# First in-projection of blocks 2 and 3: column tiles 4 to 15 as three groups of seven products, with stores, loads and conversions moved

## The chip, the cores and the metric

The program runs on one core of one Trainium2 chip. Its engines run side by side, each with a queue of its own: TensorE (PE) multiplies, VectorE (DVE), ScalarE (ACT) and GpSimd (POOL) do elementwise work, and SyncE (SP) issues the transfers. The metric is the device time of one execution in microseconds; of several runs the median counts. A time below is one on the span of the profiled execution, from its start, unless it is said to be otherwise.

## The reference

Attention with an exponentially decaying state (retention), then an MLP with a squared ReLU, then a gated MLP on normalized rows, all in float32:

```python
for t in range(S):
    state = gamma[None, :, None, None] * state + np.einsum('bhd,bhe->bhde', k[:, :, t], v[:, :, t])
    y[:, :, t] = scale * np.einsum('bhd,bhde->bhe', q[:, :, t], state)
...
h = np.maximum(x @ w_in, 0.0)              # x: 3072 x 512, w_in: 512 x 2048
x = h * h @ w_out
...
rms = np.sqrt(np.mean(x * x, axis=-1, keepdims=True) + 1e-06)
xn = x / rms * rms_g
g = xn @ w_gate                            # 512 x 1536
silu = g * (1.0 / (1.0 + np.exp(-g)))
val = xn @ w_val
return silu * val @ w_out
```

## The kernel before

The 3072 tokens go in six blocks of 512, each of four chunks of 128. A float32 matrix product is made of three passes: every operand is split into a high part (a cast on ACT, `split`, L103) and a low part (a subtraction on DVE, `low`, L100), and PE adds high x high, high x low and low x high (`mm3`, `proj`). One such pass over 128 rows and 512 tokens is one matmul of 128x512.

Block 0 and block 1 go through the first MLP one by one (`block1`). Blocks 2 and 3 go through it together, and so do 4 and 5. For a pair of blocks the in-projection is written in two ways. `in_phase` takes a column tile of 128 columns after the other: 12 matmuls for each of the two blocks, then ReLU and square on ACT. `in_pair` takes four column tiles together as a 2x2 scheme (two halves of the input dimension, two blocks) with seven products P1 to P7 for eight: each product is 12 matmuls too, its weights are a unit of 512 KB (a sum or difference of quarters of the weights, high and low part), and its other operand is one of seven combinations X[P1] to X[P7] of the blocks (`first_x` makes them, two at 128x1024 for each: a cast `xop` on ACT, a low half on DVE, with differences `raw<-raw` on DVE between them). DVE then adds what a product gives to several results: `act<-pr` behind P2, `act<-ph` or `act<-pb` behind P7, `act<-pa` behind P3. With NCL = 4, column tiles 0 to 7 are plain, and 8 to 15 are the groups 2 and 3.

Units are made once: weights arrive as 64-bit numbers (`raw`), are converted (`tick`: a magnitude on ACT, L228, and two integer operations on DVE, L233 and L234), split, and stored to DRAM as they are (`keep_units`, `keep_in`: P1, P2, P4) or as sums (`made_units`: P5, P7, P6, P3, a `made` tile each, cast on ACT, low half on DVE, stored by SP). `in_units` makes those of the in-projection, in the order of groups 2, 3, 0, 1; for groups whose rows were stored (`rows_i`) it reads them back, for the others it adds the high and low parts (`whole_rows`, four sums on DVE). `ring` is a ring of seven tiles into which SP loads the units ahead of the products that use them. Almost all of these tiles (`w`, `raw`, `rows`, `made`, `wps`, `ring`, `xop`, `act`) come from one pool of 38 places of 4 KB a partition: a new tile takes the place of an old one and waits until all that reads or writes the old one is done, a store of it included.

Between the products of blocks 2 and 3, the eight attention chunks of blocks 4 and 5 are computed, one at each visit (`visit`, L1038): a state product (into the last columns of bank `pr`, L992; not for the last four chunks), values into `pr` (L1003, L1012), and the scores of the next chunk into a pair of free banks (L957). Around a visit ACT copies `pr` out (`raw<-pr`), DVE adds the state (`st<-st,pr`), POOL decays the state and the next values and queries (L1023, L945, L934), and DVE masks the scores (`causal`, L975 and L980), which the next visit multiplies. In `in_phase` there is a visit behind the second block of each odd column tile; in `in_pair` one behind P6 and one behind P3.

The order is written out by hand: `after1` (L1407) says what follows each half of a column tile, `after1b` (L1423) what follows each product, `late0`, `late1` and `last1` what lies in `block1`. There is no planner; the names of the places where work is put are the generators `made_in` (units), `coming_xs` (X), `back` (norm) and the list `later` (stores), which are advanced by a step at a time. SP and the engines take their queues strictly in that order.

In the gated MLP, `make_late` (L1623) makes units of the last out-projection the same way, beside the first pair of blocks.

## Time and profile before

| | us |
|---|---|
| median of 3 runs (1086.36 to 1087.31) | 1086.46 |
| the profiled execution | 1087.08 |
| its span, first to last instruction | 1085.4 |
| PE busy | 1077.3 |
| DVE busy | 792.4 |
| ACT busy | 571.7 |
| POOL busy | 76.5 |
| in-projection of blocks 2 and 3, from and to | about 228 to 336 |

A wait is put down to the engine whose signal came last. A row of a timeline gives the start, the time of the instruction, the engine (SPq: SyncE's queue), the line and the operation as result<-operands with its shape; in square brackets stands how long the engine was idle before it and who ended that. The start of one row less the start of the row before is the engine's pitch, which is shorter than the time of one instruction, since the next begins before the last has quite ended.

### The profile page before, as it was taken

The numbers are of one execution on the slowest core, as the hardware profiler recorded it, in microseconds if no ns is written. First come the engines' busy times: TensorE is split into PE (matmuls) and PEld (weight loads), VectorE is DVE, ScalarE is ACT, GpSimd is POOL, SyncE is SP. The second block draws the span as 40 slices with busy tenths as digits, with TensorE's granted clock in tenths as the row PEclk, the third lists the DMA queues.
The fourth block names the chain that finished last, engine by engine and source line by source line (L and its number), as shares of the span: only waits on it lengthen the run. The fifth ranks groups of instructions, "written<-read, shape, count | busy, mean of one in ns | idle before, by whom it ended". The sixth has DMA issues, their size and how long they took to land. (4 is left out here: it accounts for less than half of the span.)

```text
span 1085.4 us, 16696 instructions
## 1 busy us (share of the span) xinstructions
PE 1077.3 (99%) x6281; PEld 887.2 (82%) x6281; DVE 792.4 (73%) x1103; ACT 571.7 (53%) x880; POOL 76.5 (7%) x65
## 2 busy tenths in 40 slices
PE   8999999999999999999999999999999999999998
PEld 7788888888888888888888887888888888888887
DVE  6988678888758995679788887995333896433585
ACT  5777445567566557785455655453333554233442
POOL 3000143314310000000000000000000000000000
PEclk9999999999999999999999999999999999999999
DMA  9868799899999779976569979767567567555563
GB/s 359 324 213 318 242 319 383 307 383 342 395 408 349 252 276 378 375 275 247 197 230 337 377 277 365 272 208 237 194 233 250 194 212 251 194 194 195 194 213 117
DMA packets 108452, 300.87 MB, mean 277 GB/s; under 512 B 11044, under 2 KB 34364, under 8 KB 108372
## 3 DMA queue, kind: packets, MB, share of 16 engines
q1 hardware_dynamic: 108192, 299.56, 76.5%
q8 instruction: 50, 0.82, 0.3%
q10 hardware_dynamic: 180, 0.24, 0.1%
q14 instruction: 30, 0.25, 0.1%
HBM read 211.14 MB, written 88.62 MB: 276 GB/s over the span
## 5 line engine op out<-in xcount | busy, mean ns | idle before, releaser
L492 ACT CAST o<-act 128x1024 fp32r<-128x1024 f32 x101 | 105.5, 1051 | 110.1 <-DVE act L107 55.8
L100 DVE TENSOR_TENSOR o<-act,o 128x1024 fp32r<-128x1024 f32 x101 | 123.0, 1222 | 25.9 <-ACT o L492 25.9
L270 PE MATMUL ph<-o,ring 128*128 128x512 f32 x228 | 88.9, 390 | 0.0
L271 PE MATMUL ph<-o,ring 128*128 128x512 f32 x228 | 88.6, 389 | 0.0
L269 PE MATMUL ph<-o,ring 128*128 128x512 f32 x228 | 88.6, 389 | 0.0
L311 PE MATMUL ph<-xh,w_i 128*128 128x512 f32 x248 | 81.2, 390 | 0.0
L269 PE MATMUL ph<-xop,ring 128*128 128x512 f32 x192 | 75.4, 393 | 1.1 <-ACT part L114 1.0
L269 PE MATMUL pa<-xop,ring 128*128 128x512 f32 x192 | 75.0, 391 | 0.0
L269 PE MATMUL pb<-xop,ring 128*128 128x512 f32 x192 | 74.9, 390 | 0.0
L270 PE MATMUL ph<-xop,ring 128*128 128x512 f32 x192 | 74.9, 390 | 0.0
L271 PE MATMUL ph<-xop,ring 128*128 128x512 f32 x192 | 74.8, 390 | 0.0
L271 PE MATMUL pa<-xop,ring 128*128 128x512 f32 x192 | 74.8, 390 | 0.0
L270 PE MATMUL pb<-xop,ring 128*128 128x512 f32 x192 | 74.8, 390 | 0.0
L271 PE MATMUL pb<-xop,ring 128*128 128x512 f32 x192 | 74.8, 389 | 0.0
L270 PE MATMUL pa<-xop,ring 128*128 128x512 f32 x192 | 74.8, 389 | 0.0
L107 DVE TENSOR_TENSOR act<-act 128x1024 f32<-128x1024 f32 x60 | 73.3, 1221 | 0.3
L110 DVE TENSOR_TENSOR part<-pr,part 128x512 f32<-128x512 f32 x38 | 25.7, 690 | 52.5 <-ACT part L114 51.2
L770 ACT ACTIVATE t<-part 128x512 f32<-128x512 f32 x54 | 34.1, 632 | 49.7 <-DVE part L110 49.7
L114 ACT COPY part<-ph 128x512 f32<-128x512 f32 x52 | 29.9, 587 | 52.7 <-PE ph L271 52.7
L311 PEld LDWEIGHTS ph<-xh,w_i 128*128 128x128 f32 x248 | 46.5, 188 | 10.2 <-ACT w_o L132 0.4
L270 PEld LDWEIGHTS ph<-o,ring 128*128 128x128 f32 x228 | 42.8, 188 | 9.6 <-DVE o L100 0.9
L269 PEld LDWEIGHTS ph<-o,ring 128*128 128x128 f32 x228 | 42.8, 188 | 8.9
(255 smaller groups left out, 2624.6 us busy)
## 6 DMA issues: line engine op xcount, KB each, us to landing
ring<-wu SPq DMA_DIRECT2D x84, 512.0 KB, 4.3
ring<-up SPq DMA_DIRECT2D x63, 512.0 KB, 4.3
ring<-uo SPq DMA_DIRECT2D x56, 512.0 KB, 3.8
ring<-ui SPq DMA_DIRECT2D x42, 512.0 KB, 7.0
wu<-ring SPq DMA_DIRECT2D x42, 512.0 KB, 6.7
raw<-w1i SPq DMA_DIRECT2D x16, 512.0 KB, 6.9
raw<-w1o SPq DMA_DIRECT2D x16, 512.0 KB, 8.4
vkt<-vk SPq DMA_DIRECT2D x16, 512.0 KB, 6.0
```

Of the source, the lines that this page charges most:

```text
L100: eng.tensor_tensor(out=dst_l, in0=src, in1=dst_h.bitcast(F32), op=ALU.subtract)
L107: eng.tensor_tensor(out=out_, in0=a, in1=b, op=ALU.subtract)
L110: eng.tensor_tensor(out=out_, in0=a, in1=b, op=ALU.add)
L114: nc.scalar.copy(dst[:, m], acc[m])
L269: nc.tensor.matmul(acc, ah, bh, start=start, stop=False, **more)
L270: nc.tensor.matmul(acc, ah, bl, start=False, stop=False, **more)
L271: nc.tensor.matmul(acc, al, bh, start=False, stop=stop, **more)
L311: nc.tensor.matmul(h, w[:, a, k * 128:(k + 1) * 128], x[b][k], start=n == 0, stop=n == len(order) - 1)
L492: nc.scalar.copy(h, src)
L770: nc.scalar.activation(t, g, AF.Silu)
```

## The change

NCL becomes 2: column tiles 0 to 3 stay plain, 4 to 15 become the groups 1, 2 and 3. `KEPT` takes over what NCL said of the weights that are stored on their way (still tiles 8 to 15). With it move:

- the unit stores: `keep_out` begins at column tile 5 of block 0 (was 8), `keep_in` at tile 12 of block 0 (was tile 0 of block 1);
- the units: `in_units` goes 1, 2, 3, 0 (was 2, 3, 0, 1), so the rows of group 1 are summed from high and low part first;
- the ring's first loads: from tile 13 of block 1 (RING_AT, was behind the blocks), and behind both halves of a plain tile;
- the conversions: from tile 11 of block 1 (MORE_AT, was 12), in `in_phase` none at tile 2 and none ahead;
- the X operands: `first_x` makes P6 and P5 before P7, advances at both halves of tiles 2 and 3, and behind P1, P2 and P6 of the first group;
- the last units of the gated MLP: at its next to last group of the first pair of blocks `make_late` makes no step behind P5 and three behind P6 (were one and two).

```diff
--- before.py
+++ after.py
@@ -39,14 +39,15 @@
 COMING = (0, 1, 2, 5, 8, 9, 13, 16, 17, 18, 19, 20)
 AHEAD = 5
 EARLY = 24
-MORE_AT = 12
+MORE_AT = 11
 W2_SOON = 25
 X_AT = (11, 12, 17, 18, 23, 24)
 
 P2, P1, P5, P6, P7, P3, P4 = range(7)
 PQ = 128 // CB
-NCL = 4
-RING_AT = 16
+KEPT = 4
+NCL = 2
+RING_AT = 13
 EPS = 1e-06
 WARM = 10
 GAMMA = (1.0 - 2.0 ** (-5.0 - np.arange(H))).astype(np.float32).astype(np.float64)
@@ -76,7 +77,7 @@
     uo2 = [[dram.tile([128, 2, 512], F32, name=f"up{q}{k}") for k in range(7)] for q in range(NQ2)]
     wu = [[dram.tile([128, 2, 512], F32, name=f"wu{n}{k}") for k in range(7)] for n in range(NPR)]
     rows2 = [[dram.tile([128, 2, 512], F32, name=f"rows_p{q}{r}") for r in range(2)] for q in range(NQ2)]
-    kept = {(k, n): dram.tile([128, 2, 512], F32, name=f"rows_{k}{n}") for k in "io" for n in range(NCL, 2 * NQ)}
+    kept = {(k, n): dram.tile([128, 2, 512], F32, name=f"rows_{k}{n}") for k in "io" for n in range(KEPT, 2 * NQ)}
 
     ones = const.tile([128, D], F32, name="ones")
     g_sb = const.tile([128, KC], F32, name="g_sb")
@@ -130,7 +131,7 @@
         t = slot(f"w_{key[0]}{key[1]}", F32R)
         W[key] = t
         nc.scalar.copy(t[:, 0, :], f)
-        if key[1] >= 2 * NCL:
+        if key[1] >= 2 * KEPT:
             nc.sync.dma_start(kept[key[0], key[1] // 2][:, key[1] % 2, :], f)
         return lambda: low(eng or nc.vector, t[:, 1, :], f, t[:, 0, :])
 
@@ -221,7 +222,7 @@
             key = steps[i][1]
             if key[0] == "p":
                 sizes[i] = row_of(key[1])
-            elif key[0] in "io" and key[1] >= 2 * NCL and i % 3 == 0:
+            elif key[0] in "io" and key[1] >= 2 * KEPT and i % 3 == 0:
                 sizes[i] = tp.tile([128, TB], F32, tag="y", name="f")
             else:
                 sizes[i] = cf.tile([128, 512], F32, tag="f", name="f")
@@ -617,17 +618,17 @@
         yield
         sub(y[0, 0], y[0, 1], y[0, 0])
         yield
+        sub(y[0, 1], y[1, 1], y[0, 1])
+        yield
+        sub(y[1, 1], y[1, 1], y[0, 0])
+        yield
+        X[P6] = put(y[1, 1])
+        yield
         X[P5] = put(y[0, 0])
         yield
-        sub(y[0, 1], y[1, 1], y[0, 1])
+        sub(y[1, 0], y[1, 0], y[1, 1])
         yield
         X[P7] = put(y[0, 1], True)
-        yield
-        sub(y[1, 1], y[1, 1], y[0, 0])
-        yield
-        X[P6] = put(y[1, 1])
-        yield
-        sub(y[1, 0], y[1, 0], y[1, 1])
         yield
         X[P4] = put(y[1, 0], True)
         yield
@@ -1249,13 +1250,13 @@
                 prev = (f, s, j)
 
         def request(key, q):
-            if 2 * q >= NCL and q < NQ:
+            if 2 * q >= KEPT and q < NQ:
                 row_tiles[key, q] = [slot("rows") for _ in range(2)]
                 for r in range(2):
                     nc.sync.dma_start(row_tiles[key, q][r], kept[key, 2 * q + r])
 
         def whole_rows(key, q):
-            if 2 * q >= NCL:
+            if 2 * q >= KEPT:
                 yield
                 return
             rows = row_tiles[key, q] = [slot("rows") for _ in range(2)]
@@ -1280,6 +1281,12 @@
         def keep_out(f):
             keep_units(uo, f, W[("o", f)])
 
+        def keep_in(f):
+            q, r, m = f // 4, f % 4 // 2, f % 2
+            w = W[("i", f)].bitcast(F32)
+            for k, h in ((P1, 0), (P2, 1)) if r == 0 else ((P4, 1),):
+                nc.sync.dma_start(units(ui[q][k])[:, m], w[:, :, h * HALF:(h + 1) * HALF])
+
         made = all_units()
 
         def early0(f):
@@ -1289,8 +1296,10 @@
         def late0(f):
             stores()
             tick(low_first=at[0] < 5)
-            if f >= 8:
-                keep_out(f - 8)
+            if f >= 5:
+                keep_out(f - 5)
+            if f >= NF1 - 4:
+                keep_in(f - NF1 + 4)
 
         nxt = Operand(True)
         block1(0, cur, lambda c: nxt, (3, 7, 11, 14), early0, late0)
@@ -1299,19 +1308,13 @@
         cur = nxt
 
         def in_units():
-            for q in (2, 3, 0, 1):
+            for q in (1, 2, 3, 0):
                 yield from whole_rows("i", q)
                 spare = cf.tile([128, 512], F32, tag="f", name="sm")
                 for n, _ in enumerate(made_units(ui, q, row_tiles.pop(("i", q)), lambda: spare, True)):
                     if n == 1:
                         request("i", q + 1)
                     yield
-
-        def keep_in(f):
-            q, r, m = f // 4, f % 4 // 2, f % 2
-            w = W[("i", f)].bitcast(F32)
-            for k, h in ((P1, 0), (P2, 1)) if r == 0 else ((P4, 1),):
-                nc.sync.dma_start(units(ui[q][k])[:, m], w[:, :, h * HALF:(h + 1) * HALF])
 
         xs, raws1 = [], []
         made_in = in_units()
@@ -1332,9 +1335,10 @@
                 next(made, None)
 
         def late1(f):
-            if f < 8:
-                keep_out(f + 8)
-            keep_in(f)
+            if f + NF1 - 5 < NF1:
+                keep_out(f + NF1 - 5)
+            if f + 4 < NF1:
+                keep_in(f + 4)
             if f % 2:
                 next(made, None)
 
@@ -1354,8 +1358,6 @@
                 more_steps(W2_SOON)
             if f > MORE_AT:
                 tick()
-            if f == 2:
-                request("i", NCL // 2)
             if f >= 4:
                 next(made_in, None)
             if f in (10, 12, 14):
@@ -1407,17 +1409,18 @@
         def after1(f, t):
             if t == 0:
                 stores()
-                tick(ahead=f < 8)
+                if f != 2:
+                    tick(ahead=False)
                 if f and f % 2 == 0:
                     next_chunk()
             elif f % 2:
                 kv, _ = visit(at_chunk, pa, True)
                 after_visit(at_chunk, sink2(at_chunk), kv)
-            if t:
+            if t or f > 1:
                 next(coming_xs, None)
             if f % 2 == 0 or t == 0:
                 next(made_in, None)
-            if t and f and len(ring) < 7:
+            if (t or f) and len(ring) < 7:
                 more_ring()
 
         def after1b(n, k):
@@ -1433,14 +1436,14 @@
                 after_visit(at_chunk, sink2(at_chunk), kv)
             if k in (P1 if n < NQ - 1 else P2, P5, P7, P4):
                 next(made_in, None)
+            if n == NCL // 2 and k in (P1, P2, P6):
+                next(coming_xs, None)
             if n == NQ - 1 and k in (P2, P6, P3):
                 i = (P2, P6, P3).index(k)
                 out_1.hi(i)
                 out_1.lo(i)
 
         in_phase(xs, lambda f: W[("i", f)], after1, between1)
-        for _ in coming_xs:
-            pass
         for n in range(NCL // 2, NQ):
             in_pair(n, after1b)
         for a in last_square:
@@ -1635,7 +1638,7 @@
 
                 def second():
                     nonlocal coming
-                    make_late(1 if p == NPR - 3 else 2)
+                    make_late({NPR - 3: 1, NPR - 2: 3}.get(p, 2))
                     if p == 0 and due:
                         sums(pb[1])
                     background()
@@ -1656,7 +1659,7 @@
                         next(coming, None)
                         next(coming, None)
 
-                pair(s, p, first, lambda: make_late(1), second, third)
+                pair(s, p, first, lambda: make_late(int(p < NPR - 2)), second, third)
 
             def store(dh, t, y):
                 nc.sync.dma_start(out[2 * s + t, dh], y)
```

Three places in the engines' order, as the programs have it. A name's number is that of a buffer. First **DVE, from column tile 3's visit to the add behind P2 of the first group**. Before (the first group is that of tiles 8 to 11, so the column tile ahead of it is 7):

```order
L100 TENSOR_TENSOR xop<-raw,xop 128x1024
L975 TENSOR_TENSOR causal<-pa_226,seen_sb 128x4x64
L980 TENSOR_TENSOR causal<-pa_226,seen_sb 64x2x64 x2
L975 TENSOR_TENSOR causal<-pa_227,seen_sb 128x4x64
L980 TENSOR_TENSOR causal<-pa_227,seen_sb 64x2x64 x2
L233 TENSOR_SCALAR f<-f 128x512
L234 SCALAR_TENSOR_TENSOR f<-raw,f 128x512
L107 TENSOR_TENSOR rows<-rows,sm 128x2x256
L100 TENSOR_TENSOR made<-sm,made 128x2x256
L110 TENSOR_TENSOR act<-pr_232,act 128x512
L110 TENSOR_TENSOR act<-pr_233,act 128x512
```

After (the first group is that of tiles 4 to 7):

```order
L108 TENSOR_TENSOR raw<-raw 128x1024
L976 TENSOR_TENSOR causal<-pa_226,seen_sb 128x4x64
L981 TENSOR_TENSOR causal<-pa_226,seen_sb 64x2x64 x2
L976 TENSOR_TENSOR causal<-pa_227,seen_sb 128x4x64
L981 TENSOR_TENSOR causal<-pa_227,seen_sb 64x2x64 x2
L101 TENSOR_TENSOR wps<-rows,wps 128x512
L234 TENSOR_SCALAR rows<-rows 128x512
L235 SCALAR_TENSOR_TENSOR rows<-raw,rows 128x512
L101 TENSOR_TENSOR made<-rows,made 128x2x256
L101 TENSOR_TENSOR xop<-raw,xop 128x1024
L111 TENSOR_TENSOR act<-pr_232,act 128x512
L111 TENSOR_TENSOR act<-pr_233,act 128x512
```

The add into `act` stood behind one conversion, one difference and one made unit; now a weight row's low half (`wps`) and an x operand's (`xop`) stand there too, and the x operand that stood ahead of the mask is a difference.

In the same place **ACT**, with the engines and transfers (DMAHW) whose signal each row waits for, before:

```order
L302 COPY raw<-pr_232 128x2x128 [waits PE_49]
L302 COPY raw<-pr_233 128x2x128 [waits PE_49]
L103 CAST xop<-raw 128x1024 [waits DVE_49]
L114 COPY act<-ph_230 128x512 [waits PE_49]
L114 COPY act<-ph_231 128x512 [waits PE_49]
L103 CAST made<-sm 128x2x256 [waits DVE_49]
L114 COPY act<-ph_230 128x512 [waits DMAHW1_49,PE_49]
L114 COPY act<-ph_231 128x512 [waits PE_49]
```

and after:

```order
L303 COPY raw<-pr_232 128x2x128 [waits PE_49]
L303 COPY raw<-pr_233 128x2x128 [waits PE_49]
L115 COPY act<-pb_228 128x512 [waits DVE_49,PE_49]
L115 COPY act<-pb_229 128x512 [waits PE_49]
L104 CAST wps<-rows 128x512 [waits DMAHW6_49]
L229 ACTIVATE rows<-raw 128x512
L104 CAST made<-rows 128x2x256 [waits DVE_49,Activation_49]
L104 CAST xop<-raw 128x1024
L104 CAST xop<-raw 128x1024 [waits DVE_49]
```

The cast of the made unit still waits for DVE, and it is followed by two x operands (X[P7], X[P4]).

Then **SP, around the store of the low and high half of a weight row (`up_154<-wps`)**, at column tile 3; before:

```order
L1344 DMA ring_2933<-ui_99 128x1024
L147 DMA up_146<-wps 128x2x256
L147 DMA up_152<-wps 128x2x256
L199 DMA rows_p_209<-rows 128x1024
L199 DMA rows_p_210<-rows 128x1024
L217 DMA raw<-w2g 128x1024
L1344 DMA ring_2995<-ui_98 128x1024
L147 DMA up_154<-wps 128x2x256
L158 DMA ui_86<-made 128x1024
```

and after:

```order
L218 DMA raw<-w2g 128x1024
L1348 DMA ring_2883<-ui_95 128x1024
L913 DMA qnt<-qT 128x512
L918 DMA kTt<-kT 128x512
L905 DMA vkt<-vk 128x1024
L1348 DMA ring_2951<-ui_96 128x1024
L148 DMA up_154<-wps 128x2x256
L1348 DMA ring_2982<-ui_97 128x1024
L159 DMA ui_107<-made 128x1024
L159 DMA ui_109<-made 128x1024
```

Three ring loads stand around that store in place of one.

Last **DVE, from P6's visit to the add behind P3 of the second group** of the new program, which is the first of the old one; before:

```order
L233 TENSOR_SCALAR f<-f 128x512
L234 SCALAR_TENSOR_TENSOR f<-raw,f 128x512
L100 TENSOR_TENSOR made<-rows,made 128x2x256
L110 TENSOR_TENSOR act<-ph_230,act 128x512
L110 TENSOR_TENSOR act<-ph_231,act 128x512
L233 TENSOR_SCALAR f<-f 128x512
L234 SCALAR_TENSOR_TENSOR f<-raw,f 128x512
L110 TENSOR_TENSOR act<-pa_226,act 128x512
L110 TENSOR_TENSOR act<-pa_227,act 128x512
```

and after:

```order
L234 TENSOR_SCALAR f<-f 128x512
L235 SCALAR_TENSOR_TENSOR f<-raw,f 128x512
L108 TENSOR_TENSOR sm<-sm,rows 128x512
L101 TENSOR_TENSOR made<-rows,made 128x2x256
L111 TENSOR_TENSOR act<-ph_230,act 128x512
L111 TENSOR_TENSOR act<-ph_231,act 128x512
L234 TENSOR_SCALAR f<-f 128x512
L235 SCALAR_TENSOR_TENSOR f<-raw,f 128x512
L108 TENSOR_TENSOR rows<-rows,sm 128x2x256
L101 TENSOR_TENSOR made<-sm,made 128x2x256
L111 TENSOR_TENSOR act<-pa_226,act 128x512
L111 TENSOR_TENSOR act<-pa_227,act 128x512
```

Three steps of made units have come in: two differences and a low half.

## Rows read from the trace of the kernel before

**Rows 1.** the page, part 1: busy us (share of the span) xinstructions, by engine

```profile
PE 1077.3 (99%) x6281; PEld 887.2 (82%) x6281; DVE 792.4 (73%) x1103; ACT 571.7 (53%) x880; POOL 76.5 (7%) x65
```

**Rows 2.** waits of PE: engine, line, who ended it: us in total, times, longest

```profile
PE ph L957 <- DMA stage<-qk: 1.4, 1, 1.4
...
PE pr L1003 <- issue: 0.2, 1, 0.2
```

**Rows 3.** windows: us, then each engine's busy us, clock, DMA share and GB/s

```profile
100.00:228.00 128.00, 128.00 (x1174) 105.54 (x1173) 99.17 (x169) 67.33 (x121) 36.47 (x28) 1.00 0.88 316
228.00:288.00 60.00, 60.00 (x539) 49.24 (x538) 52.69 (x83) 39.54 (x70) 18.43 (x13) 1.00 0.97 361
```

**Rows 4.** line L311: its matmuls on x operands, ns min/median/max, first and last

```profile
L311 PE MATMUL ph<-xop,w_i x192: 387/390/500, 228.8 to 284.4; 128*128 128x512 f32 x192
```

**Rows 5.** timeline of PE, two products of the second group

```profile
325.51 0.39 PE L269 MATMUL pb<-xop,ring 128*128 128x512 f32 x1
...
328.23 0.39 PE L269 MATMUL pa<-xop,ring 128*128 128x512 f32 x1
```

**Rows 6.** timeline of PE, the visit at column tile 3

```profile
256.47 0.69 PE L992 MATMUL pr<-vkt 128*64 128x64 f32 x16
...
258.45 0.85 PE L957 MATMUL pa<-qnt,kTt 64*64 64x128 f32 x32
259.23 0.96 PE L311 MATMUL ph<-xop,w_i 128*128 128x512 f32 x3
```

**Rows 7.** timeline of DVE, column tiles 2 and 3 and behind that visit

```profile
252.67 1.79 DVE L100 TENSOR_TENSOR made<-sm,made 128x512 fp32r<-128x512 f32 x1
254.39 1.21 DVE L107 TENSOR_TENSOR raw<-raw 128x1024 f32<-128x1024 f32 x1
255.52 0.68 DVE L107 TENSOR_TENSOR sm<-sm,rows 128x512 f32<-128x512 f32 x1
...
259.70 0.42 DVE L110 TENSOR_TENSOR st<-st,pr 128x256 f32<-128x256 f32 x1
...
261.82 0.41 DVE L975 TENSOR_TENSOR causal<-pa,seen_sb 128x256 f32<-128x256 f32 x1
...
263.10 0.60 DVE L980 TENSOR_TENSOR causal<-pa,seen_sb 64x128 f32<-64x128 f32 x2
```

**Rows 8.** timeline of POOL, the same stretch

```profile
252.31 1.61 POOL L408 TENSOR_TENSOR y<-y 128x512 f32<-128x512 f32 x1 [1.17 <-ACT y L405]
...
263.01 1.04 POOL L945 TENSOR_TENSOR vkt<-vkt,vdec_sb 128x512 f32<-128x512 f32 x1
```

**Rows 9.** timeline of ACT, column tiles 3 to 7

```profile
257.12 0.62 ACT L103 CAST made<-sm 128x512 fp32r<-128x512 f32 x1 [0.93 <-DMA rows_p<-rows]
...
259.33 1.06 ACT L103 CAST xop<-raw 128x1024 fp32r<-128x1024 f32 x1
...
286.01 0.68 ACT L228 ACTIVATE f<-raw 128x512 f32<-128x512 f32 x1 [2.63 <-DMA wq<-f]
```

**Rows 10.** timeline of DVE, the old first group, P5 to P3

```profile
302.80 0.43 DVE L233 TENSOR_SCALAR f<-f 128x512 int32<-128x512 int32 x1 [2.21 <-ACT f L228]
...
303.88 0.68 DVE L100 TENSOR_TENSOR made<-rows,made 128x512 fp32r<-128x512 f32 x1
...
306.86 1.28 DVE L110 TENSOR_TENSOR act<-pa,act 128x512 f32<-128x512 f32 x2
```

**Rows 11.** timeline of PE, the visits behind its P6 and P3

```profile
296.16 1.21 PE L1003 MATMUL pr<-causal,vkt 128*64 128x128 f32 x16 [0.22 <-issue]
...
308.47 0.85 PE L957 MATMUL pa<-qnt,kTt 64*64 64x128 f32 x32
```

**Rows 12.** timeline of all engines, gated units, behind P6 of the fifth group

```profile
653.40 0.63 ACT L103 CAST made<-rows 128x512 fp32r<-128x512 f32 x1
...
653.92 1.08 ACT L114 COPY part<-ph 128x512 f32<-128x512 f32 x2
...
654.57 0.50 PE L269 MATMUL ph<-xop,ring 128*128 128x512 f32 x1 [0.96 <-ACT part L114]
```

4 lines of the change are left out of this document (2 added, 2 removed).

## The prediction

> **What bounds the kernel now.** I read the engines' busy time first [rows 1]: TensorE (PE) is busy 1077.3 of 1085.4 us, VectorE (DVE) 792.4. Then PE's waits [rows 2]: the longest in the whole span is 1.4 us, at its start, and in the stage that changes the only one is 0.2 us. So a matmul less is time less, a wait of PE more is time more, and nothing later gives it back. Then the stage itself, the in-projection of blocks 2, 3, in a window over its column tiles, beside one over the block before [rows 3]: PE runs without a gap in both; DVE is busy 52.69 of 60 us while the column tiles run, and the DMA engines are all but full (0.97). The reader should see three resources there: PE sets the end, DVE has an eighth of its time left, the DMA queue hardly any. The question is whether the gain on PE survives on those two.
>
> The sum is made against the profiled execution's 1087.08 us (span 1085.4 and 1.68 around it); the median of the three runs is 0.62 lower, and I take that off at the end. A measurement of this kernel can tell 0.2%, 2.2 us, from no change, so "same" is 1084.3 to 1088.6.
>
> **The matmuls.** Column tiles 4 to 7 go: 4 tiles, 2 token blocks, 12 matmuls each, 96 of the 192 of [rows 4]. Seven products of 12 come: 84. Twelve matmuls take 2.72 us (325.51 to 328.23, [rows 5]), so **-2.72**. The eight visits of attention chunks stay, with 2.85 us each where a state is added (a turn of 0.09, then 256.47 to 259.23, [rows 6]); two of them move from column tiles 5 and 7 to behind P6 and P3 of the new first group.
>
> **The path to the first visit of the new group.** Let V be the end of the visit at column tile 3 (259.23 before). P1, P2 and P6 follow, and then a visit that writes the banks pr, which DVE must have read (the add of P2 into `act`) by V + 3 x 2.72 + 0.09 = V + 8.25. The visit carries a state, whose first matmuls write pr's second bank, so both halves of the add must be done.
>
> What DVE has queued ahead of that add is in the order of the changed kernel: the last rows are difference, mask, low half of a weight row, conversion, low half of a made unit, low half of an x operand, add. Before, the state's add started at V + 0.47, at 259.70 [rows 7]. Between the first column visit's mask and it the change puts one more x operand and one more difference (1.13 each at DVE's pitch, 254.39 to 255.52) and takes away one conversion with its low half (1.65): 0.6 later, so I put it at V + 1.0. Then 0.34 for it, 1.13 difference, 1.88 mask (261.82 to 263.70), 0.60 low half, 1.14 conversion (1.08 at its pitch, [rows 10]): V + 6.1. ScalarE (ACT) may write the high half of the made unit only now: its tile takes the place of the raw weights that the conversion reads, and its row in the order waits for DVE. That high half and the x operand's behind it take 1.6 (0.52 and 1.06, [rows 9, 12]): V + 7.7. Low half of the operand 1.13, add 1.29: V + 10.1. PE waits 1.9 us, with nothing in the way.
>
> Two things are in the way in this very stage. DVE and GpSimd (POOL) hold each other up: a low half that takes 0.68 took 1.79 (252.67) while POOL's sum of the norm ran [rows 7, 8], so 1.1; in this stretch POOL has a state, two decays and the last sum of the norm. I take two of 1.1: +2.2. And ACT waits for transfers, 0.93 and 2.63 us [rows 9]: a tile is overwritten only when its store has landed. SyncE's queue now has three 512 KB unit loads within five entries of such a store, where it had one, on DMA engines that are all but full. I take one wait like the longer: +2.6. So **+6.7**. Below it, the bare work: from the first column visit's state to the add DVE has 19.4 us at its pitch, and PE needs 48 matmuls, a visit and three products, 21.9 us, so with no wait at all it is 0. Above, two more holds: 8.9.
>
> The Trainium skill, GPSIMD Engine Reference, section Specifications, says that GpSimd shares its SBUF interfaces with VectorE and meets DVE instructions that have two SBUF inputs. By that all four POOL operations of the stretch would find one, 4.4 instead of 2.2, and the sum would be 2.2 us higher. The trace agrees in part: the decay at 263.01 ran its 1.04 beside the last masks, which read a bank of PSUM, and neither was held, so I stay with two.
>
> **P3 of the first group.** The scores of the visit behind P3 write banks pa, which DVE reads in the add behind P3. From the end of the visit before, PE needs 3 x 2.72 and 2.07 (258.45 less 256.47, and the turn): 10.23. DVE has state 0.34, norm 0.2, mask 1.88, low half 0.60, conversion 1.05, two unit-row sums 1.2, add 1.2, conversion 1.05, two sums 1.2, add 1.29: 10.0, begun 0.47 behind the visit, so it ends 0.25 late where all else fits. Before, the scores had 0.33 us to spare (307.50 + 0.64 against 308.47) after 2.21 us of idle DVE [rows 10, 11]. One hold of 1.1 makes it **+1.3**; bounds 0 and 2.5.
>
> **The second group.** Behind its P6, PE was held 0.38 us already (296.16, where the matmul before had ended its turn at 295.78, [rows 11]). DVE has one conversion and one sum more there (1.05, 0.72) and no x operand (1.13): +0.6. Up to its P3 DVE has three made-unit steps more, 1.8 us; the 2.21 us that it idled was a wait for ACT, which converts only when PE's P5 has been read, so it doesn't cover them, and the spare 0.33 does: +1.2 with some luck on ACT's side. Together **+1.8**, bounds 0.3 and 3.5.
>
> **The gated units, 300 us later.** At 654.57 PE waits 1.0 us because ACT casts a made unit before it empties bank ph [rows 12]. The change moves that cast behind both copies; ACT's pitch for one is 0.52 (653.40 to 653.92). **-0.5**, bounds -1.1 and 0.
>
> **At nothing.** Unit stores, ring loads and conversions that move into the blocks before: PE is busy 128.00 of 128 us there [rows 3] and waits for none of them; DVE's four sums for the new group's unit rows, 2.6 us, lie there too. In SyncE's queue the weight loads stand behind the moved stores. If that cover were gone it would be one more transfer wait, 0.9 to 2.6.
>
> Sum: -2.72 + 6.7 + 1.3 + 1.8 - 0.5 = +6.6, 1093.7 against the profiled run, **1093.0** against the median.
>
> **The rivals.**
> *DVE keeps up.* Its place is the add of P2 in the new group. The pitch sum 19.4 against 21.9 and 7.3 idle us in 60 speak for it; the serial chain through ACT speaks against. It decides if the mask behind column tile 3 ends by V + 2.4, since 5.8 us of chain follow. Then 1087.08 - 2.72 - 0.5 - 0.62 = 1083.2, at most 1084.3: faster.
> *The bare chain alone*, no hold, no transfer wait: -2.72 + 1.9 + 0.3 + 0.6 - 0.5 = -0.4, 1086; with a hold or two 1088: no change.
> *The DMA queue.* Every unit load of the new group comes into that stretch (7 x 512 KB), and a second and third wait like the 2.63 fall on ACT: 1093.0 + 5.3 = 1098.
> *The clock.* The trace grants 1.00 [rows 3], and an unbroken wait of 6 us does not occur in it [rows 2]. If the clock fell to its lower level of 1.2 GHz behind such a wait, each 512-column matmul would take 0.227 us more, 5.4 for two products: 1098. The Trainium skill, TensorE: Matmul & The Clock Gate, Part 1, says that an idle array is gated to 1.2 GHz; no row here shows it.
>
> **How the numbers follow.** Forecast 0.50 (1088.6 to 1097), DVE keeps up 0.13, bare chain 0.15, DMA queue 0.15, clock 0.07. Faster 0.13, same 0.15, slower 0.72. The range leaves out the first rival and the last part of the two longest: 1085.0 to 1099.0.
>
> **What would show it.** In the profile after: PE with 12 matmuls fewer, column-tile matmuls on `xop` x96. A wait of PE at the visit's state matmuls for DVE's add into `act`, some 5 to 7 us, or shared with a wait for ACT's copies at P2; waits at the scores into pa for DVE's add, one or two of 1 to 2 us; DVE nearly without idle time between the first column visit and the second group. The wait near 654 about halved. I am wrong if PE's waits in the stage stay under 1 us (then DVE had the room), if the longest is for a ring load, or if PE's clock shows less than 1.00.

## The result and the profile after

The changed kernel takes 1102.93 us (median of 4 runs, 1102.41 to 1103.71), the kernel before 1086.88 in the same comparison: a ratio of 1.0147, 95% interval 1.0134 to 1.0159, so 16 us slower. The forecast was 1093.0, with a range of 1085.0 to 1099.0: the direction was right, the size was not. The profiled execution has a span of 1100.7 us, 15.3 more than before.

The page's first part, by engine, to be held against [rows 1]:

```profile
PE 1079.6 (98%) x6269; PEld 887.8 (81%) x6269; DVE 799.7 (73%) x1109; ACT 574.3 (52%) x879; POOL 74.9 (7%) x65
```

PE has 12 instructions fewer and is yet busy 2.3 us longer: its matmuls got slower somewhere. Its idle time (span less busy) went from 8.1 to 21.1 us, 13.0 more. PE's waits, to be held against [rows 2] (engine, line, who ended it: us in total, times, longest):

```profile
PE pr L993 <- issue: 5.9, 1, 5.9
PE pa L958 <- issue: 3.5, 2, 2.6
PE pr L270 <- ACT raw L303: 2.4, 1, 2.4
...
PE pr L1004 <- issue: 1.0, 1, 1.0
PE ph L270 <- DVE part L111: 0.7, 1, 0.7
PE ph L270 <- ACT part L115: 0.5, 1, 0.5
```

The first four are in the stage of the change, the last two with the gated units. Windows over the stage (us; each engine's busy us; PE's clock; DMA share; GB/s), to be held against [rows 3]:

```profile
228.00:262.00 34.00, 34.00 (x284) 27.59 (x282) 23.96 (x37) 20.01 (x33) 8.41 (x6) 1.00 1.04 406
262.00:300.00 38.00, 28.71 (x254) 23.07 (x254) 27.98 (x52) 19.55 (x33) 9.98 (x9) 0.91 0.83 297
300.00:340.00 40.00, 36.29 (x310) 29.22 (x310) 25.74 (x42) 26.27 (x41) 8.18 (x6) 0.96 0.97 352
```

The column tiles lose nothing; all is lost from 262 on, in the first two groups, and the granted clock is below 1.00 in both windows. From the first matmul on `xop` (228.56; 228.80 before) to the end of the last visit (347.70; 332.66 before) the stage takes 119.14 us and took 103.86: 15.28 more, which is the whole difference of the two spans. This length of the stage is given for other runs below, since it leaves out what differs from run to run elsewhere. PE's timeline there (start, us, instruction, in brackets the wait before it):

```profile
264.44 0.50 PE L270 MATMUL pr<-xop,ring 128*128 128x512 f32 x1 [2.36 <-ACT raw L303]
...
276.06 1.12 PE L993 MATMUL pr<-vkt 128*64 128x64 f32 x16 [5.88 <-issue]
...
277.69 1.98 PE L1004 MATMUL pr<-causal,vkt 128*64 128x128 f32 x16
...
281.42 0.50 PE L270 MATMUL pa<-xop,ring 128*128 128x512 f32 x1
...
292.88 0.40 PE L958 MATMUL pa<-qnt,kTt 64*64 64x128 f32 x2 [0.90 <-issue]
...
306.39 1.21 PE L1004 MATMUL pr<-causal,vkt 128*64 128x128 f32 x16 [0.95 <-issue]
...
321.50 2.10 PE L958 MATMUL pa<-qnt,kTt 64*64 64x128 f32 x32 [2.63 <-issue]
```

In that order: the first group's P2, the visit behind its P6 and the product behind that visit, the scores behind its P3, the visit behind the second group's P6, the scores behind its P3. Two things are to be seen. The waits stand where the prediction put them, plus one at P2. And behind the two longest, work takes twice as long: the visit's values take 1.98 us (1.09 in the same visit of e5, below), the scores 2.10 (0.85 in [rows 6]). PE's clock by itself says the same (busy us, clock, DMA):

```profile
276.00:280.00 4.00, 3.94 (x48) 0.50 0.30 109
322.00:324.00 2.00, 1.95 (x31) 0.50 0.88 285
```

0.50 is the lower of the two levels, 1.2 GHz. The Trainium skill, TensorE: Matmul & The Clock Gate, Part 1, says that an idle array is gated to 1.2 GHz; the trace agrees behind the waits of 5.88 and 2.63 us, and does not behind the 2.36, where the clock stays at 1.00.

What holds the add of P2 back is a chain over four engines. DVE, from column tile 3 on:

```profile
260.21 0.43 DVE L234 TENSOR_SCALAR rows<-rows 128x512 int32<-128x512 int32 x1 [3.98 <-ACT rows L229]
...
264.76 0.42 DVE L111 TENSOR_TENSOR st<-st,pr 128x256 f32<-128x256 f32 x1 [1.06 <-ACT raw L303]
...
268.11 1.47 DVE L101 TENSOR_TENSOR wps<-rows,wps 128x512 fp32r<-128x512 f32 x1
269.51 1.49 DVE L234 TENSOR_SCALAR rows<-rows 128x512 int32<-128x512 int32 x1
...
274.67 1.29 DVE L111 TENSOR_TENSOR act<-pr,act 128x512 f32<-128x512 f32 x2
```

ACT in the same stretch:

```profile
259.52 0.66 ACT L229 ACTIVATE rows<-raw 128x512 f32<-128x512 f32 x1 [4.06 <-DMA up<-wps]
...
262.35 0.62 ACT L104 CAST made<-sm 128x512 fp32r<-128x512 f32 x1 [1.22 <-DMA ui<-made]
...
264.03 0.63 ACT L303 COPY raw<-pr 128x256 f32<-128x256 f32 x2
```

SyncE and POOL:

```profile
251.35 0.38 SPq L148 DMA_DIRECT2D up<-wps  x1
```

```profile
266.75 1.28 POOL L409 TENSOR_TENSOR y<-y 128x512 f32<-128x512 f32 x1
268.00 1.04 POOL L946 TENSOR_TENSOR vkt<-vkt,vdec_sb 128x512 f32<-128x512 f32 x1
269.00 1.71 POOL L935 TENSOR_TENSOR qnt<-qnt,qdec_sb 128x512 f32<-128x512 f32 x1
```

A store of 256 KB that was issued at 251.35 landed 8.1 us later. ACT may not write the next row of weights before, waits 4.06 us, then 1.22 for another store, and copies the visit's values out of pr at 264.03, 5.0 us behind the visit's end (V = 259.05). P2 writes pr and waits 2.36 for that. DVE starts on the state at V + 5.7, where the prediction had V + 1.0; its mask is followed by a low half that took 1.47 us and a shift that took 1.49, beside POOL's decays; and the add ends at 275.96, V + 16.9, where the prediction had V + 14.9.

### The profile page after: what moved, and what is told of

Same layout as the page of the kernel before. It is cut to its first block, busy times and chain, and to the rows that moved or that the text cites. A ratio compares the mean times of both kernels' runs of the same rounds, so it can differ in the third digit from the quotient of the medians.

```text
span 1100.7 us, 16687 instructions
## 1 busy us (share of the span) xinstructions
PE 1079.6 (98%) x6269; PEld 887.8 (81%) x6269; DVE 799.7 (73%) x1109; ACT 574.3 (52%) x879; POOL 74.9 (7%) x65
## 4 chain that ended last, share of the span: by engine, by line
PE 83%; DMA 7%; DVE 5%; ACT 2%; issue 2%; POOL 0%; SPq 0%; DVEq 0%; ACTq 0%
PE ph L270 9%; PE ph L271 9%; PE ph L272 9%; PE pa L270 8%; PE ph L312 7%; PE pa L272 7%; PE pa L271 7%; PE pb L270 5%; PE pb L272 5%; PE pb L271 5%; PE pr L270 3%; PE pr L272 3%; PE pr L271 3%; PE pr L1004 1%; DMA q<-wq 1%
## 5 line engine op out<-in xcount | busy, mean ns | idle before, releaser
L270 PE MATMUL pb<-xop,ring 128*128 128x512 f32 x208 | 81.3, 391 | 0.0
L272 PE MATMUL pb<-xop,ring 128*128 128x512 f32 x208 | 81.0, 389 | 0.0
L271 PE MATMUL pb<-xop,ring 128*128 128x512 f32 x208 | 81.0, 389 | 0.0
L108 DVE TENSOR_TENSOR act<-act 128x1024 f32<-128x1024 f32 x64 | 78.2, 1221 | 0.3
L270 PE MATMUL pa<-xop,ring 128*128 128x512 f32 x200 | 78.2, 391 | 0.0
L272 PE MATMUL pa<-xop,ring 128*128 128x512 f32 x200 | 77.9, 389 | 0.0
L271 PE MATMUL pa<-xop,ring 128*128 128x512 f32 x200 | 77.8, 389 | 0.0
L312 PEld LDWEIGHTS ph<-xh,w_i 128*128 128x128 f32 x248 | 46.5, 188 | 10.2 <-ACT w_o L133 0.4
```

The lines of the kernel that those rows point to most:

```text
L108: eng.tensor_tensor(out=out_, in0=a, in1=b, op=ALU.subtract)
L270: nc.tensor.matmul(acc, ah, bh, start=start, stop=False, **more)
L271: nc.tensor.matmul(acc, ah, bl, start=False, stop=False, **more)
L272: nc.tensor.matmul(acc, al, bh, start=False, stop=stop, **more)
L312: nc.tensor.matmul(h, w[:, a, k * 128:(k + 1) * 128], x[b][k], start=n == 0, stop=n == len(order) - 1)
```

## The experiments

Times are medians; "changed" is the changed kernel's 1102.93, "before" the kernel before, 1086.6 to 1087.8 in these comparisons. That spread of 1.2 us is also what a difference between runs of two comparisons can be off by.

**e1_busy and e5_busy20: what the slow clock costs.** Matmuls that nobody reads, into free banks, while PE would wait for the add.

```
...
-        both(P6, main, False)
+        both(P6, main, False, 20 if busy_at.pop(n, None) else 0)   # e1: 24 whenever n == 1
```

> The changed kernel with 24 more matmuls of 512 columns into the free banks ph, behind product P6 of the first group: they run while PE would wait 5.9 us for DVE's add, and what they write is overwritten by the visit's scores. They are 24 x 0.2267 = 5.4 us of work, no more than the wait. If the clock's fall behind that wait is what stretches the visit (276.06 to 281.42, 5.36 us, where the same visit takes 2.85), the granted clock stays 1.00 there, the visit takes about 2.9 and the kernel gains some 2.5 us: 1100.4. If the visit was long for another reason (its operands late, banks still being read), nothing is gained: 1102.9, and if the matmuls push the add back, 1103 to 1106.

Measured 1107.33. The condition n == 1 also holds in the in-projection of blocks 4, 5, where 24 matmuls lie on the path: 5.4 us of the time are this edit's own, and 1101.9 is left, too blurred to judge by. So it was made again, for the first in-projection alone.

> The changed kernel with 20 matmuls of 512 columns into the free banks ph behind product P6 of the first group of this in-projection alone (the earlier run of this kind put 24 of them into the second in-projection too, 5.4 us on the path there). They are 4.5 us of work inside PE's wait of 5.9. If an idle PE is what lowers the clock behind that wait, the clock is 1.00 in the visit, which then takes 2.9 us and not 5.4: the kernel gains up to 2.5, 1100.4, less whatever a fall behind the earlier wait of 2.4 costs in the same run. If the clock falls for another reason, 1102.9 or a little more.

Measured 1100.68, 2.25 less than changed. The same visit in PE's timeline:

```profile
276.39 0.69 PE L998 MATMUL pr<-vkt 128*64 128x64 f32 x16 [1.37 <-issue]
...
277.36 1.09 PE L1009 MATMUL pr<-causal,vkt 128*64 128x128 f32 x16
...
279.65 0.50 PE L270 MATMUL pa<-xop,ring 128*128 128x512 f32 x1
```

It starts 0.33 later than in the changed kernel and is over 1.77 earlier: 3.26 us for 5.36. The add came no sooner; only the clock differs. So one fall costs 2.1 us, and the same visit takes 3.26 in e2 and e9 too, where the clock is 1.00 with no matmuls added. That it was an idle PE, and not late operands, is shown for this wait.

**e2_no_tick: fewer steps ahead of the add.**

```
-                if f != 2:
+                if f < 2:
                     tick(ahead=False)
...
-            if k in (P1, P5, P7, P4):
+            if k in (P5, P7, P4) or k == P1 and n > 1:
                 tick(ahead=False)
...
-            if n < 6:
+            if n < 8:
```

> The changed kernel without the conversion steps at column tile 3 and behind P1 of the first group; the two steps are made up for 100 us later, in the out-projection. Theory of the chain: ACT has no raw magnitude there that waits for the store of up (4.06 us), so the wait at P2 (2.36) goes, and DVE has a low half and a conversion less ahead of the add of P2, so the 5.88 falls to 1 to 3 and the clock stays at 1.00: -6 to -9, 1094 to 1097. Rival, DVE and ACT are simply late from the steps before: the waits change by no more than the 2.5 us of work that was taken out, with the clock still falling: 1100. If the wait is for the ring's loads, no change: 1102.9.

Measured 1094.78 (1090.65 to 1096.86, its runs differ by more than those of the others): -8.2, inside the first theory's range. The wait at P2 is gone, the visit waits 3.2 us and not 5.9, a little more than the 1 to 3 expected, and the clock is 1.00 from 262 to 300:

```profile
270.71 0.69 PE L993 MATMUL pr<-vkt 128*64 128x64 f32 x16 [3.23 <-issue]
```

```profile
262.00:300.00 38.00, 33.13 (x309) 26.62 (x311) 30.95 (x57) 22.47 (x35) 12.32 (x11) 1.00 0.85 291
```

So a wait of 3.23 us had no fall behind it, where in the same run one of 1.88, behind the second group's P3, had. The two steps hold some 3.5 us of DVE's work, ACT's share beside it; more than twice as much came back.

**e3_scores: the two waits behind P3.**

```
-                kv, _ = visit(at_chunk, (ph, pb)[(n + 1) % 2] if k == P6 else pa, True)
+                kv, _ = visit(at_chunk, (ph, pb)[(n + 1) % 2], True)
```

> The changed kernel with one thing moved: the scores of the visit behind P3 go to the pair of banks that the group's main product doesn't use (ph or pb in turn) and no longer to pa, which DVE's add of P3 still reads. By the theory that these two waits are for that add, the 0.9 us behind the first group's P3 and the 2.6 behind the second's go, with the clock's fall behind the second (about 2.0): -4 to -5.5, 1097.4 to 1099; the mask must then be read before the next group's P1, which may give 0 to 1.5 back. If PE waited there for something else (the operands of the chunk, the decay on POOL), nothing changes: 1102.9.

Measured 1097.23: -5.7, a little more than expected. Neither wait is left, nor the fall of the clock behind the second; two new ones for the mask (1.69 and 0.50 us) take their place in part. So both waits were for DVE's add of P3 into `act`, which reads the bank that the scores write. The stage is 4.4 us shorter in the profiled execution (114.73), as expected; the rest of the 5.7 lies outside it, where the edit changes nothing.

**e4_ring11: is it the DMA queue?**

```
-RING_AT = 13
+RING_AT = 11
```

> The changed kernel with the seven ring loads begun two column tiles earlier in the block before (from tile 11, not 13), so that five of them are issued before the stage and two between its column tiles. Rival, the DMA queue: the store of up no longer lands late, ACT doesn't wait 4.06 us, the state's copy comes in time and with it all of the first group's waits go: -8 to -10, 1093 to 1095. Theory of the chain: only the wait at P2 goes or halves (2.36 to 0 or 1), and the visit behind P6 still waits 4 to 6 us for the add, because masks, low halves, conversion and POOL's holds still lie ahead of it: -1 to -2.5, 1100.4 to 1102.

Measured 1102.30, -0.6: not to be told from changed, and less than either theory expected. ACT no longer waits for the store of up, the copies come in time and the wait at P2 is gone; the visit behind P6 itself waits even longer (PE's waits):

```profile
PE pr L993 <- issue: 6.4, 1, 6.4
PE pa L958 <- issue: 3.6, 2, 2.7
```

DVE shows why: its state's add now starts at 262.45 (V + 3.8), since two steps ahead of it ran beside POOL's sum of the norm, 1.51 and 1.78 us where they take 1.22 and 0.68 elsewhere:

```profile
258.61 1.51 DVE L101 TENSOR_TENSOR xop<-raw,xop 128x1024 fp32r<-128x1024 f32 x1 [1.94 <-ACT act L453]
260.04 1.78 DVE L108 TENSOR_TENSOR rows<-rows,sm 128x512 f32<-128x512 f32 x1
```

```profile
257.76 3.50 POOL L409 TENSOR_TENSOR y<-y 128x512 f32<-128x512 f32 x2
```

PE's waits up to that visit are 6.45 us together, for 8.24, so the late store cost 1.8 of them. The kernel gains less, because the clock's fall behind the second group's P3 lasts longer here: from the start of the scores to the end of the product behind them it takes 7.0 us (319.05 to 326.09), and 5.6 in the changed kernel (321.50 to 327.14). The late store explains the wait at P2, but most of the waiting stays without it: the DMA queue alone is not the cause.

**e6_late_only: the gated units alone.** The kernel before with the two edited calls of `make_late`, and nothing else.

```
-                    make_late(1 if p == NPR - 3 else 2)
+                    make_late({NPR - 3: 1, NPR - 2: 3}.get(p, 2))
...
-                pair(s, p, first, lambda: make_late(1), second, third)
+                pair(s, p, first, lambda: make_late(int(p < NPR - 2)), second, third)
```

> The kernel before with the gated units' schedule of the changed kernel and nothing else. Forecast of the prediction: the wait near 654 (ACT empties ph behind a cast) halves, -0.5, 1086.1. Rival, the step that now runs third at one place puts DVE's add late there, and the gain is given back: 1086.6 to 1087.1.

Measured 1086.83 against 1087.45: ratio 1.0000, interval 0.9992 to 1.0008. The wait near 654 is gone from its profile, but a gain of up to 0.9 us can't be told from none. In the changed kernel the wait is 0.49 and a new one of 0.69, for DVE's add into `part`, stands 6.4 us behind it.

**e7_no_pool: POOL's share.** Its two decays behind P1 of the first group are left out.

```
...
-                next_chunk()
+                next_chunk((n, k) == (NCL // 2, P1))   # True: no decay of values and queries
```

> The changed kernel without POOL's two decays behind P1 of the first group (values of one chunk, queries of the next: they are left undecayed, which is all that is left out). If POOL's work lengthens DVE's beside it, the low half at 268.11 (1.47, alone 0.69) and the shift at 269.51 (1.49, alone 0.42) shrink by 1.85, the add of P2 ends so much earlier, the wait of 5.88 falls to 4.0, and the clock falls for less time: -1.9 to -3.5, 1099.5 to 1101. If the two were long because of the full DMA engines or their tiles, nothing changes: 1102.9.

Measured 1100.97, -2.0. On DVE:

```profile
268.29 0.69 DVE L101 TENSOR_TENSOR wps<-rows,wps 128x512 fp32r<-128x512 f32 x1
268.90 0.42 DVE L234 TENSOR_SCALAR rows<-rows 128x512 int32<-128x512 int32 x1
...
273.00 1.29 DVE L111 TENSOR_TENSOR act<-pr,act 128x512 f32<-128x512 f32 x2
```

0.69 and 0.42 for 1.47 and 1.49: the two decays held DVE for 1.85 us, shown. What that is worth in time is less clear: in the profiled execution (1102.24, the slowest of four) the clock fell behind a wait of 2.52 at P2 as well, which the changed kernel's did not. The Trainium skill, GPSIMD Engine Reference, section Specifications, has GpSimd contend for the shared SBUF interfaces with DVE instructions in a 2-port mode or with two SBUF inputs; the trace agrees: the low half (two SBUF inputs) and the shift were held, the masks, which read a bank of PSUM, at 0.42 and 0.58 were not, though POOL's last sum ran beside them. Whether the shift ran in such a mode the trace does not show.

**e9_add_first: the same work in another order.** The conversion, the made unit and the x operand behind P1 of the first group go behind P2.

```
-            if k in (P1, P5, P7, P4):
+            if k in (P2 if n == NCL // 2 else P1, P5, P7, P4):
                 tick(ahead=False)
...
-            if k in (P1 if n < NQ - 1 else P2, P5, P7, P4):
+            if k in (P1 if NCL // 2 < n < NQ - 1 else P2, P5, P7, P4):
                 next(made_in, None)
-            if n == NCL // 2 and k in (P1, P2, P6):
+            if n == NCL // 2 and k in (P2, P6, P5):
                 next(coming_xs, None)
```

> The changed kernel with the same work in another order: what stands behind P1 of the first group (a conversion with its low half, a made unit, an x operand) is put behind P2, that is behind DVE's add of P2; the two x operands after it move one product on. Theory of the queue ahead of the add: with state, difference and mask alone ahead of it, the add ends 4 to 6 us sooner, the visit's wait of 5.88 falls to 0 to 2 and the clock stays at 1.00 there; the wait at P2 (2.36, ACT behind a store) stays, and up to 2 us come back at P5: -5 to -7.5, 1095.5 to 1098. Rival, DVE has simply too much to do in the group, wherever it stands: the wait moves to P6's or P5's banks with its size, 1101 to 1103.

Measured 1097.42, -5.5. The visit behind P6 has no wait at all, with not one step left out; the 2.47 at P2 stay, as expected. The size of DVE's work is not the cause, its order ahead of the add is. But the scores behind the same group's P3 now wait 3.31 us (0.90 in the changed kernel), and 1.9 follow in the second group, with a fall of the clock behind each: part of the delay moved on to the next bank that DVE reads.

**e8, e10, e12 to e15: can the matmuls' gain come through?** Every edit that the runs so far had shown to help, together: no conversion at column tile 3 nor behind P1 of the first group (made up for in the out-projection), e9's order, e3's scores, the mask as DVE's first step behind each product, and in e8 the conversion of P7 behind the add of P3.

```
...
         def after1b(n, k):
+            mask()
             background()
-            mask()
...
-            if k in (P1, P5, P7, P4):
+            if k in (P5, P4) or k == P1 and n > 1 or k == P3:      # e8
+            if k in (P5, P4) or k in (P1, P3) and n > 2 or n == 2 and k == P1:      # e10
+            if k in (P5, P4) or (n, k) in ((2, P2), (2, P3)) or n > 2 and k in (P1, P7):      # e12 to e14
+            if k in (P5, P4) or (n, k) == (2, P2) or n > 2 and k in (P1, P7):      # e15
                 tick(ahead=False)
...
-            if k in (P1 if n < NQ - 1 else P2, P5, P7, P4):
+            if k in (P2, P5, P7, P4):      # e12 to e15; e8 and e10 as in e9
                 next(made_in, None)
```

> The changed kernel with what the runs so far point to, put together. No conversion at column tile 3 and behind P1 of the first group (made up for in the out-projection); the x operand and the made unit behind P1 go behind the add of P2; the conversion of P7 goes behind the add of P3; the scores behind P3 go to the free pair of banks, and the mask is DVE's first step behind each product. Theory of the chain: the queues ahead of the four adds are then shorter than PE's products, no wait over 1 us is left in the stage, the clock stays at 1.00, and the 2.72 us of matmuls come through but for about 1 us: 1084.5 to 1086. If DVE and the transfers were short of room as a whole, and not badly ordered, the waits come back elsewhere: 1088 to 1092.

Measured 1088.36, ratio 1.0011 (1.0002 to 1.0020). Three waits are left, 1.44, 0.71 and 1.44 us; the clock is 1.00 throughout. That is in the rival's range: the waits did come back elsewhere, though smaller. Two more conversions were taken out:

> The reordered kernel of e8 with two more conversion steps taken out of the groups (behind P3 of the first and of the second; four in all are made up for in the out-projection, behind products where no add follows). In e8 three waits were left: 1.44 for the mask behind the first group's P3 with that conversion ahead of it, 0.71, and 1.44 for a decay whose load stood behind conversions' loads and stores. Theory: the first goes, since the conversion ahead of the mask is gone, and the third shrinks with 1.5 MB less of transfers in the stretch: 1085.5 to 1087, 0 to 0.2% faster than before. If the DMA engines are the next bound, the 1.44 stays or grows: 1087.5 to 1089.

Measured 1090.49: worse, and above both ranges. The wait for the mask went, that for the add of P2 of the second group is 1.19, and the one for the decay of the queries grew to 2.28, with a fall of the clock behind it. Whether the reordering helps without the new group was the question of e11, the kernel before with the scores and the mask moved:

> The kernel before with two of the same edits: scores behind P3 into the free banks, and the mask as DVE's first step behind each product. Its groups have one wait of 0.38 us: the most that this can give is -0.4, and the mask behind P3 may cost up to 1: 1086.5 to 1088. It says whether what e8 and e10 gain is the new group's or would be had without it.

Measured 1087.68, ratio 1.0004 (0.9995 to 1.0013): nothing. In the kernel before, where PE hardly waits in the stage, these two edits have nothing to take away.

> The reordered kernel of e8 with the two conversions that stood ahead of a late step moved again: the one behind P3 of the first group goes to the out-projection (the mask has no conversion ahead of it), those behind P1 of the second group go behind its add of P2, as in the first. Theory of the queue ahead: of e8's three waits the 1.44 for the mask and the 0.71 for the add of P2 go, the 1.44 for the queries' decay stays: 1088.4 - 2.1 = 1086.3. Rival, each step that is moved makes another late by as much: 1088 to 1090.

Measured 1091.25: the theory's waits went, as it said, and the time rose, by more than the rival said. One wait is left in the whole stage, three times as long as in e8, and the clock falls behind it. PE, POOL and SyncE of e12:

```profile
309.74 1.56 PE L958 MATMUL pb<-qnt,kTt 64*64 64x128 f32 x32 [4.38 <-POOL qnt L935]
```

```profile
308.10 1.59 POOL L935 TENSOR_TENSOR qnt<-qnt,qdec_sb 128x512 f32<-128x512 f32 x1 [20.40 <-DMA qnt<-qT]
```

```profile
297.87 0.33 SPq L913 DMA_DIRECT2D qnt<-qT  x1
```

The queries of the next chunk, 256 KB, were asked for at 297.87, behind the visit before, and landed 10.2 us later; PE had reached the scores 4.4 us before their decay was done. With DVE out of the way, the transfers seem to be the bound; e13 and e14 test that.

e13 adds an early load to e12, for the chunks of the second group's P3 and the third group's P6 (`ask_q` is the load into a tile of `slot`, which `load_q` then takes):

```
             decay_q(at_chunk + 2, nc.gpsimd)
             at_chunk += 1
+            if early_q:      # (n, k) in ((1, P4), (2, P5))
+                ask_q(at_chunk + 2)
```

> e12 with the queries of two chunks loaded one visit earlier, into tiles of their own (behind P4 of the first group and P5 of the second). In e8 the scores behind P3 of the second group wait 1.44 us for POOL's decay of queries whose load was issued at 299.00, behind the visit before, and took 8.9 us. If that load is what bounds it, the wait goes: 1.4 under e12, 1084.9, which would be faster than before by 0.2%. If POOL or the engines' room decides, it stays: like e12; the two tiles come from the pool of all other units, so that a wait elsewhere could give 1 back.

Measured 1090.43. The wait for the queries is gone, and 6 us earlier there is another (PE, then ACT):

```profile
303.88 0.79 PE L270 MATMUL pa<-xop,ring 128*128 128x512 f32 x1 [3.02 <-ACT act L115]
```

```profile
303.24 1.07 ACT L115 COPY act<-pa 128x512 f32<-128x512 f32 x2 [2.57 <-DMA up<-wps]
```

ACT's copy goes into a tile whose store hasn't landed. If not the place of one load, but what stands in the queue at that time decides, its order should help. e14 changes that order alone, against e12:

```
-            stores()
+            if k not in (P6, P3):
+                stores()
...
                 after_visit(at_chunk, sink2(at_chunk), kv)
+                stores()
```

> e12 with one thing moved in SyncE's queue: behind P6 and P3 the visit and the loads of the next chunk (queries, keys, values) come ahead of the stores that wait there. In e12 the queries behind P6 of the second group were issued at 297.87, behind four stores of a row tile and a unit, and landed 10 us later, and PE waited 4.38 us for their decay; in e13, loaded a visit earlier, PE waited 3.02 us for a copy of ACT behind a store instead. If what is queued ahead of that load bounds the stage, PE's wait falls by 2 to 4.4 us and the clock stays at 1.00: 1085 to 1088. If the DMA engines are simply too full there, a wait of 2 to 4 us shows elsewhere (a store that ACT waits for, a unit of the ring): 1089.5 to 1091.5.

Measured 1086.53 (1086.67 before), ratio 0.9997 (0.9988 to 1.0006): 4.7 us less than e12. The queries are asked for at 294.02, ahead of five stores, and land 6.0 us later: the order on SyncE's queue was the bound in e12. One wait of 1.86 us for the mask is left, with a fall of the clock behind it.

> e14 with the conversion behind P3 of the second group moved to the out-projection as well. In e14 the one wait left in the stage is 1.86 us of the third group's P1 for the mask, with that conversion (308.02 to 309.17) ahead of the mask on DVE, and the clock falls for 3.5 us behind it, about 2 us more. If the conversion's place is the cause, the wait falls to 0.7 or less, the clock stays at 1.00 and 2 to 3 us come through: 1083.5 to 1085, faster than before by 0.15 to 0.3%. If what makes the mask late is ACT, which waits 3.88 us there for a store, the wait stays or moves: 1086 to 1088.

Measured 1085.77 against 1087.77 in the same comparison: ratio 0.9982, interval 0.9973 to 0.9990, so 2.0 us faster than before and 17 less than the changed kernel. The gain of 0.18% is inside what was expected. The stage in one window, of the kernel before:

```profile
228.00:340.00 112.00, 111.78 (x949) 91.30 (x948) 87.36 (x148) 75.15 (x125) 28.07 (x21) 1.00 0.98 370
```

of e15:

```profile
228.00:340.00 112.00, 111.57 (x947) 90.72 (x946) 83.36 (x144) 75.17 (x119) 26.44 (x21) 1.00 0.98 368
```

and of the changed kernel:

```profile
228.00:340.00 112.00, 99.00 (x846) 79.88 (x845) 77.68 (x129) 65.82 (x106) 26.56 (x21) 0.95 0.94 350
```

PE is busy 111.57 of 112 us, about as before the change (111.78), and has 12 matmuls less to do. The stage takes 101.62 us (229.17 to 330.79), 2.24 less than before; the twelve matmuls are 2.72, and e15's one wait there is 0.43. e15's edits against the changed kernel are e9's (in the second group too), e3's, e14's, the mask ahead of `background()`, and four conversions moved to the out-projection (`n < 6 or n in (8, 10, 12, 13)`).

## Why the prediction was wrong in size

The 15.3 us of span, by the two traces: -2.72 for the matmuls, +13.0 of idle PE, and 5.0 by which PE is busy longer than 12 matmuls less would make it. By the prediction's steps:

**The clock was the step that failed.** The sum put it at nothing. The prediction kept it as a rival with a chance of 0.07, beside the forecast, as if it could only happen instead, and its ground, that no wait of 6 us occurs in the trace before, no longer held for a forecast with a wait of 6.7 us in it: whoever expects that wait has to price what follows it, and the rival's own working says how (0.227 us for each matmul at the lower level). It fell twice. Behind the add of P2 it cost 2.1 (e5). Behind the second group's P3 the scores and the product's first matmuls took 3.8 us, from 321.50 to 325.30, where the same take 1.8 elsewhere: 2.0. That is 4.1 of the 5.0 by which PE is busy longer; where the other 0.9 lies was not found. The prediction's own sign of being wrong, a clock below 1.00, is what showed. But the clock alone doesn't leave the range: 1093.0 and 4.1 are 1097.1. It took the waits below as well.

**The path to the first visit: the mechanism right, its parts mis-sized.** Forecast 6.7 in one wait at the visit; measured 5.88 there and 2.36 at P2, 8.24, under the upper bound of 8.9. Inside it POOL's two holds were put at 2.2 and measured 1.85 (e7). The transfer wait was put at 2.6 and measured 4.06 and 1.22; what the prediction put "at nothing", the ring loads moved into the columns, was its cause (e4), so that cover was indeed gone. Without it PE still waits 6.45 (e4), where the prediction's own terms leave 4.1. The reason was not in the prediction: POOL's sum of the norm beside DVE's steps ahead of the state. It started the state at V + 1.0 from the spacing before [rows 7], where e4, without the late store, has V + 3.8. That the 6.7 comes within 1.5 of the 8.24 is in part luck.

**P3 of the first group**: +1.3 forecast, 0.90 and 0.15 measured. The wait is for the add named (e3). The hold of 1.1 that makes up most of the forecast did not occur: POOL's decays there ended at 284.87, beside DVE's masks, and what DVE lost was 1.69 us idle, for a cast of ACT. So the size was right by luck:

```profile
285.63 0.69 DVE L101 TENSOR_TENSOR wps<-rows,wps 128x512 fp32r<-128x512 f32 x1 [1.69 <-ACT wps L104]
```

**The second group**: +1.8 forecast, bounds 0.3 and 3.5. Behind P6 0.95 where 0.22 stood before (+0.6 forecast, +0.7 measured). Behind P3 +1.2 forecast, 2.63 measured: mis-sized by 1.4. The prediction counted no hold there, but POOL's two decays ran beside DVE's conversion and difference ahead of that add. DVE of the changed kernel, then POOL:

```profile
313.49 1.67 DVE L235 SCALAR_TENSOR_TENSOR f<-raw,f 128x512 int32<-128x512 int32 x1
315.09 1.53 DVE L108 TENSOR_TENSOR sm<-sm,rows 128x512 f32<-128x512 f32 x1
```

```profile
313.30 1.32 POOL L935 TENSOR_TENSOR qnt<-qnt,qdec_sb 128x512 f32<-128x512 f32 x1 [9.94 <-PE ph L272]
314.58 1.49 POOL L946 TENSOR_TENSOR vkt<-vkt,vdec_sb 128x512 f32<-128x512 f32 x1
```

0.69 and 0.68 are their times alone: 1.8 us of hold, enough for what was missing. It is read from the trace; no run left these two decays out.

**The gated units**: -0.5 forecast, +0.2 measured (0.96 before; 0.49 and 0.69 after). The wait did halve; the new one for DVE's add was not foreseen. Alone, the edit moves nothing that can be measured (e6).

**The matmuls**: -2.72, as forecast: PE has 12 less, those on `xop` at the columns are 96. That they are a gain where PE needn't wait is shown by e15, with a stage 2.24 us shorter.

Summed, on the two profiled executions (1087.08 and 1102.41): +6.6 forecast, +4.1 for the clock, 0.9 of longer busy time that was not placed, and +1.5, -0.25, +1.5 and +0.7 for the four terms make +15.1, of +15.3. The difference of the medians is 16.05, 0.7 more, because the changed kernel's profiled execution is the fastest of its four and the other one lies above its median.

**The range** was too narrow for one reason: each rival was priced by itself, and its upper end left out what happens when long waits, holds and the clock come together. They aren't independent: in e5, filling the wait took the fall away.

**The rivals.** "DVE keeps up" and "the bare chain" fell. "The DMA queue" came in part: ACT had a second wait for a transfer, but taking both away brought 0.6 us (e4) of the 5.3 that the rival was priced at; it is the next bound as soon as DVE's order is mended (e12 to e14). "The clock" came true, together with the forecast.

**Still open**: what makes the clock fall behind one wait and not behind a longer one (see the last section), and the 0.9 us above.

## What to carry to other kernels

Where PE is the bound, a chain that another engine must finish before PE may write a bank is priced by what is queued ahead of the read, not by that engine's busy share: with the same work behind the read instead of ahead of it (e9) the longest wait went. A forecast wait of PE should carry the price of a fall of the clock; here a fall added some 2 us to each of two waits, though a wait of 3.23 us (e2) brought none. And after mending one queue look at the next: here the order of DVE's steps, then the order of loads and stores on SyncE, each hid the one behind it.

## What the runs showed of the hardware

- The clock fell to 0.50 behind single waits of PE, among others of 1.86 us (e14), 1.88 (e2), 2.29 (e3), 2.52 (e7), 2.63 (changed) and 2.94 (e1), and not behind 2.36 (changed), 2.45 (e5), 2.47 (e9) or 3.23 (e2). So the length of a wait alone does not say whether the clock falls. In e14, PE's clock in 2 us pieces:

```profile
310.00:312.00 2.00, 1.94 (x7) 0.80 1.04 405
312.00:314.00 2.00, 2.00 (x7) 0.50 1.03 408
```

  Here the lower level is granted while PE is at work again, in the changed kernel already while it waits (0.75 from 272 to 276, with nothing on PE).
- DVE and POOL hold each other up, by about 1 us at a time: a shift of 0.42 us took 1.49 and a low half of 0.69 took 1.47 beside POOL's decays, and POOL's state decay of 0.61 us took 1.53 at 265.26, beside DVE's difference.
- With the DMA engines' share at 1.0, 256 KB took 6 to 10 us to land: a store at 251.35 8.1, the queries at 297.87 in e12 10.2, and 6.0 when they went ahead of five stores (e14). Three products of PE take as long. What depends on such a transfer has to be asked for that much earlier, and ahead of what can wait.
